# First batch's keys loaded by place and summed by matrix products; mean from an accumulated sum; idle products removed

## The chip, the cores and the metric

The kernel runs on one core of a Trainium2 chip. The metric is the time of one execution on the device in microseconds, the median of several runs; lower is better. The core's engines are named as the profile names them: PE (TensorE, matrix products), DVE (VectorE), ACT (ScalarE), POOL (GpSimd) and SP (SyncE, which here only issues transfers). Each takes its instructions strictly in the order of its own queue and waits for the others through semaphores.

## The reference

Attention over pooled keys, then a feed-forward network, both in float32:

```python
# q: 4 x 12288 x 128, kv: 4 x 384 x 32 x 128, w_sr: 128 x 128
kv_pool = kv.reshape(B, H // 4, 4, W // 4, 4, C).mean(axis=(2, 4))   # mean of 16 places
k = v = kv_pool.reshape(B, -1, C) @ w_sr                             # 768 keys a batch
s = scale * (q @ k.transpose(0, 2, 1))
a = np.exp(s - s.max(-1, keepdims=True))
a /= a.sum(-1, keepdims=True) + 1e-09
x = (a @ v).reshape(B * S, 128)
# w_in: 128 x 2048, w_out: 2048 x 128
h = x @ w_in
out = (h - np.tanh(h)) @ w_out
```

## The kernel before

The 49152 tokens are taken in 96 groups of 512, 24 to a batch. Channels lie on the 128 partitions. A group has 52 products of 512 columns on PE: six scores (L850), two shares (L878), three and six that make the weighted values (L884, L894), then sixteen forth into the 2048 inner features (L965), three linear terms (L954) and sixteen back (L1003). DVE and ACT turn each 128x1024 block of scores or inner features into its nonlinear part (L854, L857, L969, L972); one block a group is done by POOL (L979, L983). POOL also splits numbers into upper and lower parts (L888, L908, L934) and issues transfers that add (L873). ACT writes the group's result (L1014).

Ahead of the first group stands a head, which is the place of the change:

- `words_of` (L303) turns blocks of w_in and w_out, which arrive as 64-bit words, into float32: per block, three passes on ACT (L333, L349, L352) and four on DVE (L336, L339, L343, L355). Four blocks are of w_in, four of w_out.
- `weights` transposes w_in by products with the identity (L384), copies it (L392), and multiplies it with itself (L403, L407) for a bound that is only used at the end.
- `keys(b, s0)` (L425) makes the pooled keys of batch b. For batch 0, twelve transfers of 512 KB bring 64 keys with all 16 places each (L452). DVE sums the places of eight of these blocks (L466), POOL of four, by four halving additions (L460). The sums land in `kvp` (128x768). Six small sums per batch (L502), a sum over them (L506) and a scaling (L507) give the mean key; `apart` subtracts it (L511, ACT); `centre` multiplies it with w_sr (L514, PE; L517, DVE); `product` and `product_by_key` multiply the keys with w_sr, once by channel (L521) and once by key (L530); ACT copies the outcomes (L526, L543, L534); L547 is the values' second moment. For batches 1 to 3, POOL gathers the sums with adding transfers (L437) while the batch before is computed.
- `warm` (L488) multiplies parts of `kvp` with the identity; nothing reads the outcome.
- `about_centre` (L578) expands the network around the mean: sixteen products of one column (L614), a chain of small DVE instructions on `hb` (L619 to L670), then weights scaled by the parts of `hb`: `Wg` (L732, L756, DVE and POOL), products with them (L738, L763), copies on ACT (L746, `winr`), and `Wr` (L776, POOL). The first product forth (L965) needs `winr` and the first group's `dr` (L908).

The order of all instructions is made when the program is built: class `Plan` takes each piece of work with a step and a guessed duration, and repeatedly takes the piece that its model would start first, the lower step first among those that start together. `MOVES` (L222) shifts single steps of the head and of the next batches' work; `AT` (L806) holds the steps of a group's instructions. `HELD` names the pooling step of batch 0 from which the loads of w_out and of the first queries may be issued. `BUFS` gives the number of buffers behind each name; a tile that takes a buffer waits for all readers of the old one.

Of the kernel before, what the change touches and what calls it, by code (L numbers as in the profile page):

```python
# [15 lines left out]
AF = mybir.ActivationFunctionType  # L16
# [185 lines left out]
def attention_then_ffn(ctx: ExitStack, tc: tile.TileContext, q, kv_by_key, kv_by_place, w_sr, w_in,  # L202
# [5 lines left out]
    K, W = kv_by_key.shape[1], kv_by_key.shape[2]  # L208
# [31 lines left out]

    DIRECT, HELD = 2, 6
# [182 lines left out]

    def keys(b, s0):  # L425
# [6 lines left out]
        NK = K // KB  # L432
        c = min(b, 2)
        for w in range(W if b else 0):
            def gather(w=w):
                if w:
                    PL.dma_start(out=plan[kvp], in_=kv_by_place[b - 1, w], accum_op=ALU.add)  # L437
                else:
                    SP.dma_start(out=plan[kvp], in_=kv_by_place[b - 1, w])

            put = at((b * NG - GATHER[b - 1] + max(w - 1, 0)) * UN - 17.0, "gather", c, w)
            plan.op(put - (0.01 if w else 4), *(("POOL", 0.88) if w else ("SP", 0.5)), gather, (), (kvp,),
                    late=0.81 if w else 1.0, dma=2.3 if w else 1.1)
        for j in range(0 if b else NK):
            gap = 0.1
            s, key = s0 - gap * (NK - j) - 2, f"kc.{b}.{j}"
            sb(key, ("E", "r", "rp", "kc", "r", "r")[j % 6], [P, KB, W])
            ks = slice(j * KB, (j + 1) * KB)
            s = at(s, "pool", j)

            def load(ks=ks, key=key):
                SP.dma_start(out=plan[key], in_=kv_by_key[:, ks, :])  # L452

            plan.op(s - 8, "SP", 0.5, load, (), (key,), late=2.0, dma=1.27)
            if j % 3 == 2:
                for k, w in enumerate((8, 4, 2, 1)):
                    def fold(key=key, w=w, ks=ks):
                        x = plan[key]
                        to = plan[kvp][:, ks].unsqueeze(2) if w == 1 else x[:, :, 0:w]
                        PL.tensor_tensor(out=to, in0=x[:, :, 0:w], in1=x[:, :, w : 2 * w], op=ALU.add)  # L460

                    plan.op(s + k / 8, "POOL", 0.2 + KB * w * 0.0021, fold, (key,),
                            ((kvp, j),) if w == 1 else (key,))
            else:
                def pool(key=key, ks=ks):
                    V.tensor_reduce(out=plan[kvp][:, ks], in_=plan[key], op=ALU.add, axis=AX.X)  # L466

                plan.op(s, "DVE", 1.2, pool, (key,), ((kvp, j), "held") if j == HELD else ((kvp, j),))
# [13 lines left out]
        for x, put in ((pc, sc), (pm, s3), (p4, s4)):  # L482
            bank(x, "x", put)
        if b == 0:
            big("warm", s0 - 3)
            for j in range(WN // KB - 1, NK):
                def warm(j=j):
                    PE.matmul(out=plan["warm"][:, 0:WN], lhsT=ident,  # L488
                              rhs=plan[kvp][:, (j + 1) * KB - WN : (j + 1) * KB], start=True,
                              stop=True)  # L490

                plan.op(s0 - 3, "PE", 1.2, warm, ["ident"] + [(kvp, i) for i in range(j + 1)],
                        ("warm",))
        big(pk, s1)
# [810 lines left out]
```

## Time and profile before

| | us |
|---|---|
| median of 3 runs | 1290.07 |
| lowest and highest | 1289.26, 1292.4 |
| the profiled execution's own time | 1289.32 |
| its span, first to last instruction | 1287.6 |
| first product forth (L965) starts, from the span's start | 59.70 |
| the 96 group results (L1014) start | 78.7 to 1281.0 |

The span has a head of about 60 us, in which the weights and the first batch's keys are made ready, a long body of groups, and some 6 us behind the last result. The views used below are the page (one line for each engine), windows (busy time of each engine in a stretch and the clock that TensorE was granted; 1.00 is 2.4 GHz, 0.5 is 1.2 GHz), the list of waits, and timelines. In a timeline, neighbouring instructions of one line stand in one row with their count; the bracket says how long the engine stood idle ahead and for what. A matmul of float32 operands has two records for each product, so x16 is eight products.

### The profile page before, as it was taken

Reading aid. Unit: us, or ns where it says so; the run is one execution under the profiler, and the core shown is the slowest. Engines: PE = TensorE matmul, PEld = TensorE weight load, DVE = VectorE, ACT = ScalarE, POOL = GpSimd, SP = SyncE. Lnnn points to the kernel's source line nnn. Section 1 sums busy time; section 2 is a strip of 40 time slices with the busy share of each in tenths; the row PEclk is TensorE's granted clock in tenths of the full one; section 3 lists DMA queues with packets and bytes.
Section 4 is the critical chain, followed back from the end, with each engine's and each line's share of the span. In section 5 each row is a group of like instructions: output and inputs, shape, how many; then the busy total and the mean of one; then the engine's idle time right before and its main releaser. Section 6 shows DMA issues by size and latency. Waiting matters only on the chain.

```text
span 1287.6 us, 17375 instructions
## 1 busy us (share of the span) xinstructions
PE 1257.1 (98%) x5520; PEld 879.8 (68%) x5520; DVE 1213.7 (94%) x1201; ACT 1201.0 (93%) x1423; POOL 1147.5 (89%) x969
## 2 busy tenths in 40 slices
PE   5899999999999999999999999999999999999997
PEld 4666667777676677777766667776776666666665
DVE  6899899999999999999999999999999999999996
ACT  4799999999999999999999999999999999999995
POOL 3599987999999988899999987899988988989886
PEclk8999999999999999999999999999999999999999
DMA  9367744456657543455467743444434444344431
GB/s 364 69 144 151 167 98 107 111 127 148 143 132 161 120 118 90 125 131 138 108 148 143 160 103 103 103 119 107 115 90 115 103 106 118 93 115 103 106 88 33
DMA packets 82708, 158.46 MB, mean 123 GB/s; under 512 B 9937, under 2 KB 12113, under 8 KB 82609
## 3 DMA queue, kind: packets, MB, share of 16 engines
q0 software_dynamic: 33552, 66.99, 30.7%
q1 hardware_dynamic: 49056, 90.29, 20.0%
q8 instruction: 45, 0.74, 0.2%
q14 instruction: 55, 0.44, 0.1%
HBM read 57.93 MB, written 25.39 MB: 65 GB/s over the span
## 4 chain that ended last, share of the span: by engine, by line
PE 74%; POOL 14%; DMA 4%; issue 2%; DVE 2%; ACT 2%; SPq 0%; POOLq 0%; ACTq 0%; DVEq 0%
PE big L965 23%; PE acc L1003 22%; PE big L850 8%; PE x L894 8%; PE acc L954 4%; PE x L884 4%; DMA rs<-r 3%; POOL rp L983 3%; PE x L878 3%; POOL z L983 2%; POOL z L979 2%; POOL rs L873 2%; POOL ql L888 1%; POOL dl L934 1%; DVE r L972 1%
## 5 line engine op out<-in xcount | busy, mean ns | idle before, releaser
L972 DVE SCALAR_TENSOR_TENSOR r<-big,u 128x1024 fp32r<-128x1024 f32 x672 | 788.7, 1218 | 26.8 <-ACT u L969 26.4
L969 ACT ACTIVATE u<-big 128x1024 f32<-128x1024 f32 x672 | 671.1, 1029 | 34.8 <-PE big L965 23.3
L965 PE MATMUL big<-dr,winr 128*128 128x512 f32 x1536 | 518.9, 419 | 0.7 <-DVE r L972 0.6
L1003 PE MATMUL acc<-r,Wr 128*128 128x512 f32 x1344 | 414.5, 398 | 0.6 <-DVE r L972 0.6
L857 DVE SCALAR_TENSOR_TENSOR r<-E,big 128x1024 f16<-128x1024 f32 x288 | 350.2, 1217 | 22.5 <-ACT E L854 21.8
L965 PEld LDWEIGHTS big<-dr,winr 128*128 128x128 f32 x1536 | 272.1, 188 | 118.8 <-DVE r L972 33.0
L854 ACT ACTIVATE E<-big 128x1024 f32<-128x1024 f32 x288 | 297.2, 1033 | 3.7 <-PE big L850 2.5
L1003 PEld LDWEIGHTS acc<-r,Wr 128*128 128x128 f32 x1344 | 250.0, 188 | 58.5 <-DVE r L972 1.5
L983 POOL TENSOR_TENSOR rp<-z,v 128x1024 fp32r<-128x1024 f32 x96 | 270.8, 2821 | 0.2
L983 POOL TENSOR_TENSOR z<-z,v 128x1024 f32<-128x1024 f32 x96 | 243.8, 2539 | 0.1
L873 POOL DMA_DIRECT2D rs<-r x188 | 211.2, 1124 | 7.6 <-DMA rs<-r 6.1
L979 POOL TENSOR_SCALAR z<-v 128x1024 f32<-128x1024 f32 x96 | 122.7, 1278 | 82.1 <-ACT v L976 81.8
L850 PE MATMUL big<-qr,kTr 128*128 128x512 f32 x576 | 193.0, 417 | 0.4 <-ACT winr L746 0.2
L888 POOL TENSOR_TENSOR ql<-q,qr 128x512 fp32r<-128x512 f32 x96 | 185.2, 1929 | 1.1 <-ACT qr L835 1.1
L894 PE MATMUL x<-r,vvr 128*128 128x512 f16 x576 | 174.3, 385 | 0.0
L934 POOL TENSOR_TENSOR dl<-df,dr 128x512 fp32r<-128x512 f32 x96 | 163.2, 1700 | 0.0
L850 PEld LDWEIGHTS big<-qr,kTr 128*128 128x128 f32 x576 | 101.4, 188 | 39.9 <-DVE r L972 21.9
L976 ACT COPY v<-big 128x1024 f32<-128x1024 f32 x96 | 97.5, 1016 | 8.1 <-PE big L965 1.6
L894 PEld LDWEIGHTS <-vvr 128*128 128x128 f16 x576 | 33.4, 98 | 78.6 <-issue 78.4
L908 POOL TENSOR_SCALAR dr<-df 128x512 fp32r<-128x512 f32 x96 | 81.4, 848 | 0.0
L1003 PE MATMUL acc<-rp,Wr 128*128 128x512 f32 x192 | 77.0, 482 | 3.6 <-POOL rp L983 3.6
L1014 ACT ACTIVATE o<-acc,At 128x512 f32<-128x512 f32 x96 | 65.6, 683 | 7.5 <-PE acc L1003 7.4
(184 smaller groups left out, 1029.9 us busy)
## 6 DMA issues: line engine op xcount, KB each, us to landing
rs<-r POOLq DMA_DIRECT2D x188, 256.0 KB, 3.6
q<-in_q_dram SPq DMA_DIRECT2D x96, 256.0 KB
out_dram<-o SPq DMA_DIRECT2D x96, 256.0 KB
rs<-r SPq DMA_DIRECT2D x94, 256.0 KB
kvp<-in_kv_by_place_dram POOLq DMA_DIRECT2D x45, 384.0 KB, 6.0
r<-in_kv_by_key_dram SPq DMA_DIRECT2D x6, 512.0 KB
kc<-inverse SPq DMA_DIRECT2D x12, 256.0 KB
u<-in_moe_w_in_dram SPq DMA_DIRECT2D x3, 512.0 KB
```

What stands on the lines that cost most here:

```text
L850: PE.matmul(out=half(plan[s], h), lhsT=plan[kTr][:, n * P : (n + 1) * P], rhs=plan[qr], start=True, stop=True)
L854: A.activation(out=plan[e], in_=plan[s], func=AF.Exp)
L857: V.scalar_tensor_tensor(out=plan[r], in0=plan[e], scalar=-1.0, in1=plan[s], op0=ALU.add, op1=ALU.subtract)
L873: PL.dma_start(out=plan[rs], in_=plan[r2s[k]], accum_op=ALU.add)
L888: PL.tensor_tensor(out=plan[ql], in0=plan[qs], in1=plan[qr].bitcast(F32), op=ALU.subtract)
L894: PE.matmul(out=plan[num], lhsT=plan[vvr][:, n], rhs=half(plan[f"r2.{g}.{k}"], h), start=(start and h == 0), stop=(stop and h == 1))
L934: PL.tensor_tensor(out=plan[dl], in0=plan[df], in1=plan[dr].bitcast(F32), op=ALU.subtract)
L965: PE.matmul(out=half(plan[hp], h), lhsT=plan[winr][:, f * P : (f + 1) * P], rhs=plan[dr], start=True, stop=True)
L969: A.activation(out=plan[u], in_=plan[hp], func=AF.Square)
L972: V.scalar_tensor_tensor(out=plan[r], in0=plan[hp], scalar=1.0, in1=plan[u], op0=ALU.add, op1=ALU.mult)
L983: PL.tensor_tensor(out=plan[to], in0=plan[x], in1=plan[y], op=ALU.mult)
L1003: PE.matmul(out=plan[acc], lhsT=plan[Wr][:, 2 * n + h], rhs=half(plan[r], h), start=(start and h == 0), stop=(stop and h == 1))
```

## The change

For batch 0, the input that lay by key is gone; all four batches lie by place. Sixteen transfers of 384 KB bring one place of all 768 keys each, into buffers lent from other names (`PLACES`). DVE adds the first fourteen places in seven pairs (128x768); PE multiplies the seven sums and the last two places with w_sr, all into the same accumulator, nine products of 768 columns as two of 384. `sums` copies the outcome to `kvp` on ACT and accumulates its sum in the same instruction; three DVE scalings make from it the subtrahends and the centre. So `centre` and its copy are gone for batch 0, `apart` and `copy_keys` subtract by their bias, and the values by key come from products with the identity. POOL's halving additions and the products of `warm` are gone. For batches 1 to 3, one sum over 768 columns takes the place of six small ones and the sum over them. `HELD` goes from 6 to 3, and all numbers of `MOVES` and `AT` are new.

```diff
@@ -220,25 +220,23 @@
     MOVES = {
-        "load.i.0": -22.9, "load.i.1": -18.7, "words.i.1": -54.5, "words.i.3": -7.3, "WW": -172.2,
...
+        "words.o.0": 22.9, "words.o.2": -7.3, "words.o.3": 19.1, "first.0.3": 53.8,
...
-    DIRECT, HELD = 2, 6
+    DIRECT, HELD = 2, 3
@@ -422,6 +420,8 @@
+    PLACES = ("r", "r", "r", "r", "rp", "rp", "kc", "kc", "z", "E", "u", "u", "u", "E", "r", "r")
@@ -429,43 +429,44 @@
-        for j in range(0 if b else NK):
...
-            def load(ks=ks, key=key):
-                SP.dma_start(out=plan[key], in_=kv_by_key[:, ks, :])
...
-            if j % 3 == 2:
...
-                        PL.tensor_tensor(out=to, in0=x[:, :, 0:w], in1=x[:, :, w : 2 * w], op=ALU.add)
...
-                def pool(key=key, ks=ks):
-                    V.tensor_reduce(out=plan[kvp][:, ks], in_=plan[key], op=ALU.add, axis=AX.X)
...
+        ALONE = W - 2
+        for w in range(0 if b else W):
+            place = f"place.{w}"
+            sb(place, PLACES[w], [P, K])
+
+            def load(w=w, place=place):
+                SP.dma_start(out=plan[place], in_=kv_by_place[0, w])
...
+        for j, w in enumerate(() if b else [*range(0, ALONE, 2), *range(ALONE, W)]):
+            x, y = f"place.{w}", f"place.{w + 1}"
...
+            def add(x=x, y=y):
+                V.tensor_tensor(out=plan[x], in0=plan[x], in1=plan[y], op=ALU.add)
+
+            def place_product(x=x, w=w):
+                for c in range(2):
+                    PE.matmul(out=plan[pk][:, c * G : c * G + KH], lhsT=wsr,
+                              rhs=plan[x][:, c * KH : (c + 1) * KH], start=(w == 0),
+                              stop=(w == W - 1))
...
@@ -480,32 +481,29 @@
-        if b == 0:
-            big("warm", s0 - 3)
-            for j in range(WN // KB - 1, NK):
-                def warm(j=j):
-                    PE.matmul(out=plan["warm"][:, 0:WN], lhsT=ident,
-                              rhs=plan[kvp][:, (j + 1) * KB - WN : (j + 1) * KB], start=True,
-                              stop=True)
...
-        def part(n):
-            of = plan[kvp][:, n * 2 * KB : (n + 1) * 2 * KB].rearrange("p (a k) -> p a k", a=4)
-            V.tensor_reduce(out=plan[row][:, 4 * n : 4 * n + 4], in_=of, op=ALU.add, axis=AX.X)
...
+        def sums():
+            if b:
+                V.tensor_reduce(out=plan[row][:, 24:25], in_=plan[kvp], op=ALU.add, axis=AX.X)
+            else:
+                A.activation(out=halves(plan[kvp]), in_=key_halves(), func=AF.Identity,
+                             accum_out=plan[row][:, 24:25])
 
         def mean():
...
+            for to, by in ((25, -1.0 / K), (26, -scale / (K * W)), (27, 1.0 / (K * W)))[: 1 if b else 3]:
+                V.tensor_scalar(out=plan[cen] if to == 27 else plan[row][:, to : to + 1],
+                                in0=plan[row][:, 24:25], scalar1=by, scalar2=None, op0=ALU.mult)
@@ -522,13 +520,16 @@
         def copy_keys():
...
+                A.activation(out=halves(plan[kTr]), in_=key_halves(), func=AF.Identity,
+                             bias=plan[row][:, 26:27], scale=scale / W)
...
-                          rhs=wsr, start=True, stop=True)
+                          rhs=wsr if b else ident, start=True, stop=True)
...
@@ -804,14 +810,14 @@
     AT = dict(
-        forth=[4.5, 6.4, 3.4, 2.2, 5.4, 5.7, 0.3, 2.8],
...
+        forth=[4.6, 6.0, 5.2, -0.1, 1.2, 0.44, 5.6, -0.5],
...
```

On PE, between the transposes of w_in and the first second-moment product, there stands before (`big<-kvp,ident` is `warm`, `acc<-col,win` the first-order products):

```order
L384 MATMUL big<-ident,win_67 128x128 x16
L403 MATMUL x<-winT 128x128 x16
L488 MATMUL big<-kvp,ident 128x512 x4
L514 MATMUL x<-row,wsr 128x1
L488 MATMUL big<-kvp,ident 128x512
L614 MATMUL acc<-col,win_67 128x1 x8
L416 MATMUL x<-W_208 128x128
L530 MATMUL big<-wsr,kvp 128x128 x3
L521 MATMUL big<-kvp,wsr 128x384 x2
L614 MATMUL acc<-col,win_67 128x1 x8
L850 MATMUL big<-qr,kTr 128x512 x2
L530 MATMUL big<-wsr,kvp 128x128 x3
```

and now, with the sums and single places in the buffers r, rp, kc, z and u:

```order
L382 MATMUL big<-ident,win_67 128x128 x8
L463 MATMUL big<-r,wsr 128x384 x4
L463 MATMUL big<-rp,wsr 128x384 x2
L463 MATMUL big<-kc,wsr 128x384 x2
L463 MATMUL big<-z,wsr 128x384 x2
L463 MATMUL big<-u,wsr 128x384 x4
L463 MATMUL big<-r,wsr 128x384 x4
L620 MATMUL acc<-col,win_67 128x1 x12
L531 MATMUL big<-ident,kvp 128x128 x3
L382 MATMUL big<-ident,win_67 128x128 x8
L856 MATMUL big<-qr,kTr 128x512 x2
L620 MATMUL acc<-col,win_67 128x1 x4
L531 MATMUL big<-ident,kvp 128x128 x3
L401 MATMUL x<-winT 128x128 x16
```

Half of the transposes and the product of w_in with itself stand behind the first-order products now, and four of the sixteen first-order products behind transposes and scores.

On DVE, from the scaling of the mean to the instruction that takes over the first-order products (L619 before, L625 after; `v`, `wout` and `o` are the words of w_out), there stands before:

```order
L517 TENSOR_SCALAR col<-x 128x1
L339 TENSOR_SCALAR v<-v 128x512
L343 SCALAR_TENSOR_TENSOR wout_69<-u,v 128x512
L355 ISA wout_69<-wout_69,o 128x1024
L419 TENSOR_REDUCE norms<-x 128x1
L336 TENSOR_SCALAR v<-v 128x512
L339 TENSOR_SCALAR v<-v 128x512
L343 SCALAR_TENSOR_TENSOR wout_69<-u,v 128x512
L336 TENSOR_SCALAR v<-v 128x512
L355 ISA wout_69<-wout_69,o 128x1024
L339 TENSOR_SCALAR v<-v 128x512
L619 TENSOR_SCALAR hb<-acc 128x16
```

and now:

```order
L505 TENSOR_SCALAR row<-row 128x1 x2
L505 TENSOR_SCALAR col<-row 128x1
L334 TENSOR_SCALAR v<-v 128x512
L337 TENSOR_SCALAR v<-v 128x512
L341 SCALAR_TENSOR_TENSOR wout_69<-u,v 128x512
L334 TENSOR_SCALAR v<-v 128x512 x2
L337 TENSOR_SCALAR v<-v 128x512 x2
L341 SCALAR_TENSOR_TENSOR wout_69<-u,v 128x512 x2
L353 ISA wout_69<-wout_69,o 128x1024
L334 TENSOR_SCALAR v<-v 128x512
L353 ISA wout_69<-wout_69,o 128x1024
L625 TENSOR_SCALAR hb<-acc 128x16
```

Before, two blocks of w_out are whole ahead of the `hb` row and a third is begun; now three are taken up to their third pass, two of them whole, and a fourth is begun.

On POOL, from the first `Wg` to the first group's `dr`, there stands before:

```order
L756 TENSOR_TENSOR Wg<-winT,hb 128x4x128
L732 TENSOR_TENSOR Wg<-ident,hb 128x4x128
L555 TENSOR_TENSOR Mh<-Mn,Mh 128x128
L732 TENSOR_TENSOR Wg<-ident,hb 128x4x128
L776 TENSOR_TENSOR Wr<-wout_69,hb 128x512
L437 DMA kvp<-in_kv_by_place_dram 128x768
L756 TENSOR_TENSOR Wg<-winT,hb 128x4x128 x3
L776 TENSOR_TENSOR Wr<-wout_69,hb 128x512
L437 DMA kvp<-in_kv_by_place_dram 128x768
L776 TENSOR_TENSOR Wr<-wout_69,hb 128x512
L908 TENSOR_SCALAR dr<-df 128x512
```

and now:

```order
L762 TENSOR_TENSOR Wg<-winT,hb 128x4x128
L782 TENSOR_TENSOR Wr<-wout_69,hb 128x512 x3
L738 TENSOR_TENSOR Wg<-ident,hb 128x4x128
L556 TENSOR_TENSOR Mh<-Mn,Mh 128x128
L436 DMA kvp<-in_kv_by_place_dram 128x768
L738 TENSOR_TENSOR Wg<-ident,hb 128x4x128
L762 TENSOR_TENSOR Wg<-winT,hb 128x4x128 x2
L782 TENSOR_TENSOR Wr<-wout_69,hb 128x512
L436 DMA kvp<-in_kv_by_place_dram 128x768
L762 TENSOR_TENSOR Wg<-winT,hb 128x4x128
L914 TENSOR_SCALAR dr<-df 128x512
```

Three of the four `Wr` blocks stand ahead of the diagonal `Wg` (`Wg<-ident,hb`) now, and one `Wg<-winT,hb` directly ahead of `dr`; no `Wr` stands behind `dr`.

## Rows read from the trace of the kernel before

**Rows 1.** the page: busy time (share) xinstructions, and the chain by engine.

```profile
PE 1257.1 (98%) x5520; PEld 879.8 (68%) x5520; DVE 1213.7 (94%) x1201; ACT 1201.0 (93%) x1423; POOL 1147.5 (89%) x969
...
PE 74%; POOL 14%; DMA 4%; issue 2%; DVE 2%; ACT 2%; SPq 0%; POOLq 0%; ACTq 0%; DVEq 0%
```

**Rows 2.** windows: busy of PE, PEld, DVE, ACT, POOL; then PEclk, DMA, GB/s.

```profile
10.00:20.00 10.00, 8.31 (x61) 7.82 (x60) 8.66 (x14) 4.41 (x7) 6.08 (x8) 1.00 1.03 418
...
19.00:23.00 4.00, 0.03 (x1) 0.00 (x0) 3.11 (x3) 0.27 (x1) 2.80 (x5) 1.00 1.03 421
23.00:30.00 7.00, 6.30 (x8) 2.70 (x9) 3.40 (x10) 1.85 (x3) 3.75 (x5) 0.51 1.07 389
...
40.00:43.50 3.50, 3.27 (x14) 3.17 (x15) 3.33 (x11) 1.58 (x5) 0.03 (x1) 0.51 0.21 81
...
1010.00:1240.00 230.00, 230.00 (x981) 159.15 (x980) 226.00 (x208) 225.32 (x262) 202.99 (x163) 1.00 0.42 104
```

**Rows 3.** PE's waits, whole span: total us, times, longest.

```profile
PE acc L1003 <- POOL rp L983: 3.6, 5, 1.1
PE x L547 <- ACT kc L534: 1.9, 1, 1.9
PE acc L763 <- DVE wout L355: 0.7, 1, 0.7
```

**Rows 4.** the 96 group results, line L1014: duration, first and last start.

```profile
L1014 ACT ACTIVATE o<-acc,At x96: 678/682/703, 78.7 to 1281.0; 128x512 f32<-128x512 f32 x96
```

**Rows 5.** PE's timeline: start, us, engine, line, operation, [idle before <-releaser].

```profile
13.40 2.05 PE L384 MATMUL big<-ident,win 128*128 128x128 f32 x16 [0.71 <-DVE win L355]
15.29 3.74 PE L403 MATMUL x<-winT 128*128 128x128 f32 x32
...
23.70 6.72 PE L488 MATMUL big<-kvp,ident 128*128 128x512 f32 x8 [4.67 <-DVE kvp L466]
...
31.33 1.84 PE L614 MATMUL acc<-col,win 128*128 128x1 f32 x16
...
34.01 1.46 PE L521 MATMUL big<-kvp,wsr 128*128 128x384 f32 x4
...
40.23 2.93 PE L547 MATMUL x<-kc 128*128 128x128 f32 x12 [1.85 <-ACT kc L534]
...
57.90 2.05 PE L763 MATMUL acc<-Wg,wout 128*128 128x129 f32 x16 [0.70 <-DVE wout L355]
59.70 1.19 PE L965 MATMUL big<-dr,winr 128*128 128x512 f32 x4
```

**Rows 6.** DVE's timeline, same columns.

```profile
27.90 0.29 DVE L502 TENSOR_REDUCE row<-kvp 128x4 f32<-128x128 f32 x1 [2.45 <-POOL kvp L460]
...
28.43 0.15 DVE L507 TENSOR_SCALAR row<-row 128x1 f32<-128x1 f32 x1
...
37.18 0.17 DVE L619 TENSOR_SCALAR hb<-acc 128x16 f32<-128x16 f32 x1 [0.42 <-PE acc L614]
...
37.60 0.17 DVE L639 TENSOR_TENSOR hb<-hb 128x16 f32<-128x16 f32 x1
...
56.08 0.69 DVE L905 TENSOR_TENSOR df<-x,t 128x512 f32<-128x512 f32 x1
```

**Rows 7.** POOL's timeline, same columns.

```profile
24.96 2.53 POOL L460 TENSOR_TENSOR r<-r 128x512 f32<-128x512 f32 x3 [3.01 <-DMA r<-in_kv_by_key_dram]
...
56.26 1.03 POOL L776 TENSOR_TENSOR Wr<-wout,hb 128x512 fp32r<-128x512 f32 x1 [1.85 <-DVE wout L355]
57.27 1.05 POOL L908 TENSOR_SCALAR dr<-df 128x512 fp32r<-128x512 f32 x1
```

**Rows 8.** ACT's timeline, same columns.

```profile
26.25 0.68 ACT L333 ACTIVATE v<-u 128x512 f32<-128x512 f32 x1 [6.92 <-DMA u<-in_moe_w_out_dram]
...
31.53 0.94 ACT L511 ACTIVATE kvp<-kvp,row 128x768 f32<-128x768 f32 x1 [2.69 <-PE big L488]
...
35.83 0.79 ACT L526 ACTIVATE kTr<-big 128x768 fp32r<-128x768 f32 x1
```

More of the change, by code (lines that the diff above doesn't have):

```diff
@@ L207, in attention_then_ffn @@
     B, C, N = q.shape
[L208 removed]
+    W, K = kv_by_place.shape[1], kv_by_place.shape[3]
     F = w_in.shape[1]
@@ new lines, in keys @@
+        ALONE = W - 2
[4 more added lines that the diff above has]
+                SP.dma_start(out=plan[place], in_=kv_by_place[0, w])
+            plan.op(s0 - 12 + w / 16, "SP", 0.5, load, (), (place,), late=2.0, dma=0.95)
+        if b == 0:
+            big(pk, s0 - 3)
+        for j, w in enumerate(() if b else [*range(0, ALONE, 2), *range(ALONE, W)]):
+            x, y = f"place.{w}", f"place.{w + 1}"
+            put = at(s0 - 2 + j / 16, "pool", j)
+            def add(x=x, y=y):
[5 more added lines that the diff above has]
+                              stop=(w == W - 1))
+            if w < ALONE:
+                plan.op(put, "DVE", 0.87, add, (y,), (x, "held") if j == HELD else (x,), port=True)
+            plan.op(s0 - 2 + j / 16, "PE", 1.3, place_product, ("wsr", x), (pk,), late=0.2)
@@ L482, in keys @@
         for x, put in ((pc, sc), (pm, s3), (p4, s4)):
-            bank(x, "x", put)
-        if b == 0:
-            big("warm", s0 - 3)
-            for j in range(WN // KB - 1, NK):
-                def warm(j=j):
-                    PE.matmul(out=plan["warm"][:, 0:WN], lhsT=ident,
-                              rhs=plan[kvp][:, (j + 1) * KB - WN : (j + 1) * KB], start=True,
-                              stop=True)
-                plan.op(s0 - 3, "PE", 1.2, warm, ["ident"] + [(kvp, i) for i in range(j + 1)],
-                        ("warm",))
-        big(pk, s1)
+            if b or x != pc:
+                bank(x, "x", put)
+        if b:
+            big(pk, s1)
         big(pv, s2)
@@ L556, in moment_left @@
                              op=ALU.subtract)
-        for n in range(NK // 2):
-            of = (kvp,) if b else ((kvp, 2 * n), (kvp, 2 * n + 1))
-            plan.op(sc - 0.5, "DVE", 0.3, partial(part, n), of, ((row, n),))
-        plan.op(sc, "DVE", 0.35, mean, (row,), (row,))
-        plan.op(sc, "ACT", 0.85, apart, (kvp, row), (kvp,), late=0.1)
-        plan.op(sc, "PE", 0.2, centre, ("wsr", row), (pc,), late=0.2)
-        plan.op(sc, "DVE", 0.12, copy_centre, (pc,), (cen,))
-        for c in range(2):
-            plan.op(sv[0] if c else s1, "PE", 0.65, partial(product, c), ("wsr", kvp), ((pk, c),), late=0.2)
-        plan.op(sv[0], "ACT", 0.9, copy_keys, (pk,), (kTr,), late=0.1)
+        if b:
+            plan.op(sc - 0.5, "DVE", 0.87, sums, (kvp,), (row,))
+            plan.op(sc, "DVE", 0.12, mean, (row,), (row,))
+            plan.op(sc, "ACT", 0.85, apart, (kvp, row), (kvp,), late=0.1)
+            plan.op(sc, "PE", 0.2, centre, ("wsr", row), (pc,), late=0.2)
+            plan.op(sc, "DVE", 0.12, copy_centre, (pc,), (cen,))
+            for n in range(2):
+                plan.op(sv[0] if n else s1, "PE", 0.65, partial(product, n), ("wsr", kvp), ((pk, n),),
+                        late=0.2)
+            plan.op(sv[0], "ACT", 0.9, copy_keys, (pk,), (kTr,), late=0.1)
+        else:
+            plan.op(sc, "ACT", 0.85, sums, (pk,), (kvp, (row, 0)), late=0.1)
+            plan.op(sc, "DVE", 0.4, mean, ((row, 0),), ((row, 1), cen), late=0.1)
+            plan.op(sv[0], "ACT", 0.9, copy_keys, (pk, row), (kTr,), late=0.1)
+            plan.op(at(sc, "apart"), "ACT", 0.85, apart, (kvp, row), (kvp,), late=0.1)
         for j in range(2):
-            plan.op(sv[1] if j else s2, "PE", 0.7, partial(product_by_key, j), ("wsr", kvp), ((pv, j),),
+            plan.op(sv[1] if j else s2, "PE", 0.7, partial(product_by_key, j), ("wsr" if b else "ident", kvp), ((pv, j),),
                     late=0.2)
@@ L806, in attention_then_ffn @@
     AT = dict(
-        forth=[4.5, 6.4, 3.4, 2.2, 5.4, 5.7, 0.3, 2.8],
-        first=[3.7, 6.2, 2.3, -0.8, 5.0, 5.8, -1.2, 1.38],
-        then=[-4.8, 10.1, 6.0, 3.7, 9.5, 10.0, 2.4, 5.4],
-        back=[11.5, 11.0, 7.1, 6.3, 10.16, 10.3, 5.6, 6.46], scores=[-20.8, -19.0, -20.4],
-        exps=[-22.6, -20.0, -21.2], beyond=[-18.5, -15.0, -17.6], values=[-4.7, -4.5, -3.3],
-        more=[-2.2, -1.7], num=-5.0, copied=16.8, added=[-26.1, -22.4], shares=-5.6, left=-8.4,
-        straight=-3.6, apart=-0.6, rounded=-11.8, rounded_q=-25.5, slope=5.0, result=10.5,
-        lower_q=-21.6, lower_left=-6.6)
+        forth=[4.6, 6.0, 5.2, -0.1, 1.2, 0.44, 5.6, -0.5],
+        first=[3.78, 5.9, 4.6, -0.6, 1.4, 0.7, 5.8, -1.8],
+        then=[-7.6, 8.9, 8.4, 2.5, 3.8, 2.9, 8.5, 0.91],
+        back=[9.9, 8.5, 7.86, 5.6, 7.4, 6.1, 8.2, 5.22], scores=[-21.23, -19.2, -23.4],
+        exps=[-21.2, -20.2, -23.2], beyond=[-19.6, -16.1, -20.3], values=[-3.2, -6.4, -7.1],
+        more=[-5.0, -2.9], num=-6.9, copied=-7.6, added=[-27.1, -24.8], shares=-7.6, left=-7.33,
+        straight=-3.9, apart=-1.61, rounded=-14.8, rounded_q=-25.9, slope=4.9, result=9.41,
+        lower_q=-24.5, lower_left=-9.6)
     def attention(g, s0):
```

46 lines of the change are left out of this document (13 added, 33 removed), and 30 rows, old and new, of the table MOVES.

## The prediction

> **What bounds the kernel now.** I read the page's busy line first: PE is busy for 98% of the span and carries 74% of the chain that ended last [rows 1]. The window from 1010 to 1240 us then shows that this is a true bound in the body: PE is busy for all 230.00 us at a granted clock of 1.00, with DVE at 226.00 and ACT at 225.32 close behind [rows 2]. The list of waits confirms it: over the whole span, PE's waits inside the body sum to little, the largest entry being 3.6 us in five waits for POOL's `rp` [rows 3]. So between the first result at 78.7 and the last at 1281.0 [rows 4] nothing is to be won but those few microseconds, unless PE gets fewer products. It does not: the change keeps all 52 products of a group. What can move is the head, up to the first product forth at 59.70 [rows 5].
>
> In the head I followed the timelines. PE transposes and squares w_in up to 15.29 + 3.74 = 19.03, stands idle for 4.67 us and then runs `warm` [rows 5], while the keys come in at 418 GB/s [rows 2]. The last block of keys reaches POOL at 24.96, after 3.01 us of waiting for the transfer, and POOL needs 2.53 us and a last small addition for it [rows 7]; DVE then waits 2.45 us for POOL and sums the last part at 27.90 [rows 6]. The mean, `centre` and its copy follow, and the first-order products start at 31.33 [rows 5]. `hb` is taken at 37.18 [rows 6]. So the keys' transfer, POOL's folding and the serial path of the mean set the start of the chain, and `warm` stands beside it.
>
> **The change part by part.**
>
> *Transfers.* Twelve times 512 KB and sixteen times 384 KB are the same 6.3 MB. At 418 GB/s [rows 2] a place takes 393216 / 418000 = 0.94 us. I therefore put the last place where the last block was, at about 25.0, and the last but one at 24.0. The buffers fit this: the queue brings place 14 ahead of place 13, so that the seventh pair is complete only with the last transfer but one.
>
> *Pair additions.* No 128x768 addition is in the trace. A 128x512 one took 0.69 us (L905) and a 128x16 one 0.17 (L639) [rows 6]; the slope, 0.52 us for 496 columns, gives 0.17 + 752 x 0.00105 = 0.96 us. A pair arrives every 1.9 us, so DVE keeps up, and only the last addition counts: 24.0 to 25.0.
>
> *Products.* A product of 768 columns took 1.46 us in the trace, first start to last end (L521) [rows 5]. The sum of pair seven and the two single places stand in this order in PE's queue, so three products lie behind 25.0, even though place 14 was there earlier. At 1.3 to 1.46 each they end at 28.9 to 29.4; I take 29.0, since products that follow closely overlap. These nine products replace L521 and the ten records of `warm`.
>
> *The mean.* `sums` on ACT is a 128x768 pass: 0.94 us for L511, 0.79 for L526 [rows 8]; I take 0.94, to 30.0. No accumulating pass is in the trace; I bound it by one row of the same size and by twice that (1.9 us). Three scalings at 0.15 each (L507) [rows 6] and a start to start of about 0.2 bring the centre at 30.6, and the first-order products at 30.7, where they were at 31.33. Gain: 0.6 us. POOL's folds, the six small sums, `centre` and its copy are thus gone from this path, but three products and an ACT pass have come in.
>
> *From there to `hb`.* Sixteen records (eight products) took 1.84 us [rows 5], so twelve products take 2.8, to 33.5. Then PE has three value products, eight transposes (2.05 for sixteen records [rows 5]) and a pair of scores ahead of the last four: I get 37.5 for the accumulator. But DVE's queue now has three blocks of w_out ahead of the `hb` row, and these blocks' ACT passes begin only behind `sums`, for the first of them stands behind it in ACT's queue and its transfer stands behind four loads of queries. From about 30.7, ten ACT passes at 0.55 to 0.9 a step and then two DVE passes of 0.69 give 38.3 (38.0 to 38.8). So `hb` comes 1.1 us later than at 37.18, although the mean came 0.6 earlier. Behind the waiting DVE stands everything of `hb`, and POOL and PE wait for that.
>
> *From `hb` to the first product forth.* Before, this took 59.70 - 37.18 = 22.5 us. In it POOL's `Wr` waits 1.85 us for a block of w_out, `dr` ends at 58.32 [rows 7], and PE then still has most of sixteen records of L763 (2.05 us) to do, which had waited 0.70 for another block [rows 3, 5]. Now a third block of w_out is already done before `hb`, `Wr` no longer stands late, and only half of those sixteen records (about 1.0 us) stands ahead of the first product forth; the other half has gone behind it. Between getting nothing back (+1.1: 60.8) and getting back all of the 1.0 and the 1.85 (58.0), I take 59.4, nearer to the middle, because `dr` also rests on exponentials and DVE passes that are as many as before. Net: -0.3 us.
>
> *Behind the first product forth.* Eight records of the slopes' products have moved here: +1.0 us, since PE is the bound here. The waits for `rp` sit in the first groups, where POOL issues two adding transfers in a group; now the groups with two lie partly there and partly in the middle of the batch. Bounds: all 3.6 us gone [rows 3], or as much again lost; I take 0. For batches 1 to 3, seven small DVE instructions (six of some 0.29, one of 0.18) become one of at most 0.96 us, so DVE has 0.9 us less per batch in a body where PE never waits [rows 2]; I take -0.4 in all, between 0 and -2.7.
>
> *Sum.* -0.3 + 1.0 + 0.0 - 0.4 = +0.3 us on the profiled execution's 1289.32 us, that is 1289.6. The median of the runs is 0.75 above that execution, so the forecast means "no change".
>
> **TensorE's clock without `warm`.** After PE had done next to nothing from 19 to 23 us (0.03 us busy), its granted clock in the next window is 0.51, the lower of the two levels, and it is 0.51 again from 40 to 43.5, where a wait of 1.85 us for ACT had just ended [rows 2, 3, 5]. So a short idle time can cost the full clock. In the changed head PE has products from about 14 us on, one for each 1.9 us at 1.3 to 1.46, that is some 70% of the time, and then a gap from 29.0 to 30.7. The Trainium skill ("TensorE: Matmul & The Clock Gate", section "HAM oscillation — how this bites in real kernels") describes a loop whose bursts of products are shorter than the wait for the next data, and which found the throttle on again at every burst. By that rule all nine products would run at the lower level; here the bursts are longer than the waits, so I hold it for unlikely, and take the sum at the full clock up to 29.0.
>
> **The rivals.**
>
> *Clock lost at the end of the keys (slower).* Place: the last three products and the first-order products. At the lower level four 512-column products took 6.72 us (L488) [rows 5], so 768 columns take 1.5 x 1.68 = 2.52 us, and three of them 3.6 us more than at 1.3. Twelve first-order products would take up to 2.8 us more, of which 0.8 hides behind DVE's words. It decides when the clock falls before about 25 us: +3.6 to +5.6, so 1293.2 to 1295.2; if it only falls in the gap at 29, +2, so 1291.6. For it speak the two windows at 0.51, against it that PE's longest idle time ahead of 25 us should be some 1.5 us. With all nine products at the lower level, 14.4 + 9 x 2.52 = 37.1 instead of 29.0: +8, 1297.7, which is where the rule named above leads.
>
> *The body's waits go, and the head comes out short (faster).* If POOL's new order takes away the 3.6 us of waits for `rp`, and the head gets back what I called possible (58.0), the time is 1289.6 - 3.6 - 1.4 = 1284.6. For it speaks that DVE and POOL have less to do; against it that the transfers which POOL issues are as many.
>
> *POOL's pairs of transfers in mid-batch (slower).* Each new group with two of them could hold `rp` back by 0.7 us, the mean of the five waits [rows 3]. Five such groups cost +3.5: 1293.1. Against it: in the full window POOL is busy for only 203 of 230 us [rows 2].
>
> *The change does not do what it says.* If transfers of many small buffers go slower, say 389 instead of 418 GB/s [rows 2], the last place comes 1.0 us later: 1290.6. This counts as no change.
>
> **How the numbers follow.** Forecast and near variants, with the transfer case: 0.55. Clock lost: 0.19, of which about 0.12 lands above the bound, 0.03 of it the case of all nine. Waits gone: 0.18, nearly all of it faster. Pairs in mid-batch: 0.08, half above the bound. A measurement of this kernel can tell about 0.3% from no change, that is 3.9 us: faster below 1286.2, slower above 1293.9. Faster 0.20, same 0.63, slower 0.17. The range goes from the low rival, 1284.6, to the clock's upper case without the nine, 1295.0.
>
> **What would show it.** Right: adds of about 0.96 us on DVE, the last ending near 25; three products behind it with a PE clock of 1.00; the first-order products near 30.7; `hb` near 38.3, behind a pass of the words; the first product forth near 59.4; 95 periods between first and last result as long as before, 1281.0 - 78.7 = 1202.3. Wrong, if the clock in the windows from 14 to 31 us is near 0.5, if the accumulating pass takes near 1.9 us, if `rp` waits stand in the middle of a batch, or if the periods of the body differ by more than 2 us in sum.

## The result and the profile after

The changed kernel is slower: 1303.59 us (median of 6 runs, 1302.64 to 1304.74) against 1291.02 us for the kernel before in the same comparison, a ratio of 1.0099 with a 95% interval of 1.0086 to 1.0112. The forecast was "no change", 1289.6 us with a range up to 1295.0; the time lies above it. The profiled execution took 1303.50 us, its span is 1301.7 us.

The page's busy line, and the row of the 96 results (L1020 now, to set beside [rows 4]):

```profile
PE 1265.2 (97%) x5540; PEld 885.0 (68%) x5540; DVE 1210.0 (93%) x1176; ACT 1204.2 (93%) x1425; POOL 1136.8 (87%) x953
```

```profile
L1020 ACT ACTIVATE o<-acc,At x96: 675/683/693, 79.4 to 1295.1; 128x512 f32<-128x512 f32 x96
```

The first result comes at 79.4 instead of 78.7, the last at 1295.1 instead of 1281.0. So of the 14 us between the two spans the head up to the first result holds 0.7 and the body, first result to last, 13.4 (1215.7 against 1202.3). POOL has less to do and is idle longer. PE's waits in the whole span (line, releaser, total us, times, longest), to set beside [rows 3]:

```profile
PE acc L1009 <- POOL rp L989: 11.0, 15, 1.6
PE big L382 <- DVE win L353: 10.3, 1, 10.3
PE acc L620 <- DVE col L505: 1.3, 1, 1.3
PE big L744 <- DVE r L863: 0.9, 1, 0.9
```

The waits for `rp` went from 3.6 us in five to 11.0 us in fifteen. That list counts only idle time, and it rests on ends of products that the profile models. Counted from start to start instead, each product against the median for the same pair of neighbours (delays over 0.15 us), the products of `rp` are late by about 5 us in 6 groups before and by about 20 us in 27 groups after. The difference, some 14 to 15 us, covers the whole loss of the body. Summed by groups, from the starts of the results:

| groups | before, us | after, us |
|---|---|---|
| 0 to 12 | 155.0 | 158.7 |
| 12 to 24 | 155.8 | 157.2 |
| 24 to 36 | 154.2 | 155.5 |
| 36 to 48 | 153.6 | 158.1 |
| 48 to 60 | 154.2 | 155.6 |
| 60 to 72 | 152.8 | 153.1 |
| 72 to 95 | 276.7 | 277.4 |

From group 60 on, where POOL gathers no more keys, the two hardly differ. So the loss seems to need the gathering transfers (e3 below tests it), and yet the order of PE's products in a group is, by their kind, the same as before. The way from one to the other shows in POOL's timeline of the first group behind 79 us, before first, then after (start, us, engine, line, operation, [idle before <-releaser]):

```profile
83.15 2.56 POOL L983 TENSOR_TENSOR z<-z,v 128x1024 f32<-128x1024 f32 x1
85.52 1.04 POOL L873 DMA_DIRECT2D rs<-r  x1
86.16 2.85 POOL L983 TENSOR_TENSOR rp<-z,v 128x1024 fp32r<-128x1024 f32 x1
```

```profile
84.02 2.87 POOL L989 TENSOR_TENSOR z<-z,v 128x1024 f32<-128x1024 f32 x1
89.40 0.89 POOL L879 DMA_DIRECT2D rs<-r  x1 [2.52 <-DMA rs<-r]
90.04 2.65 POOL L989 TENSOR_TENSOR rp<-z,v 128x1024 fp32r<-128x1024 f32 x1
```

A group has three `r2` blocks (128x1024, DVE's outcome of the scores), and `rs` is their sum: SP copies one of them to `rs`, and POOL issues two transfers that add the others. The first of these stands between the two multiplications that make `rp`. It must wait until SP's copy of the block `r2s[0]`, the first by number, has landed. After the change it waits 2.52 us for that, with `rp` behind it in the queue. The block that it adds, the last of the three, was done five microseconds earlier, at 84.25 (DVE's L863, 83.03 + 1.22). SP's queue says why the copy is late, again before and after:

```profile
79.45 0.36 SPq L1017 DMA_DIRECT2D out_dram<-o  x1
79.91 0.47 SPq L870 DMA_DIRECT2D rs<-r  x1
```

```profile
80.14 0.36 SPq L1023 DMA_DIRECT2D out_dram<-o  x1
82.31 0.47 SPq L876 DMA_DIRECT2D rs<-r  x1
```

Before, the copy follows the result's store at once. After, it stands 2.2 us behind it, because it waits for DVE. DVE's making of the first two blocks, before, then after:

```profile
78.05 1.21 DVE L857 SCALAR_TENSOR_TENSOR r<-E,big 128x1024 f16<-128x1024 f32 x1
...
80.38 1.22 DVE L857 SCALAR_TENSOR_TENSOR r<-E,big 128x1024 f16<-128x1024 f32 x1
```

```profile
78.49 1.21 DVE L863 SCALAR_TENSOR_TENSOR r<-E,big 128x1024 f16<-128x1024 f32 x1
...
81.06 1.22 DVE L863 SCALAR_TENSOR_TENSOR r<-E,big 128x1024 f16<-128x1024 f32 x1 [0.23 <-ACT E L860]
```

The new `AT` makes the third block of scores first (its `beyond` step is -20.3, that of the first block -19.6; before they were -17.6 and -18.5). `copied` still takes `r2s[0]`. Before, that was the block made first, ready at 79.26; now it is the group's second, ready at 82.28, and the copy is issued that much later. In a group without gathering transfers it mostly still lands in time; beside them it held POOL until 89.4.

In the head, PE's timeline after, to set beside [rows 5]:

```profile
25.58 2.74 PE L463 MATMUL big<-r,wsr 128*128 128x384 f32 x8
29.63 2.84 PE L620 MATMUL acc<-col,win 128*128 128x1 f32 x24 [1.30 <-DVE col L505]
32.33 0.91 PE L531 MATMUL big<-ident,kvp 128*128 128x128 f32 x6
33.08 3.35 PE L382 MATMUL big<-ident,win 128*128 128x128 f32 x16
...
60.57 1.18 PE L971 MATMUL big<-dr,winr 128*128 128x512 f32 x4
```

and the windows (busy us of PE, PEld, DVE, ACT, POOL, then granted clock, DMA share, GB/s):

```profile
19.00:23.00 4.00, 4.00 (x14) 2.27 (x12) 1.56 (x2) 0.00 (x0) 0.00 (x0) 1.00 1.03 413
23.00:30.00 7.00, 4.86 (x18) 2.57 (x16) 1.23 (x4) 2.16 (x5) 1.26 (x1) 1.00 1.07 392
30.00:40.00 10.00, 10.00 (x75) 9.86 (x75) 7.65 (x23) 8.84 (x15) 0.00 (x0) 0.83 0.26 84
```

The clock stays at 1.00 through all place products. It falls to 0.50 at 33.4 us, just after L382 has begun, and the sixteen records of L382 take 3.35 us, where sixteen such records took 2.05 before [rows 5].

### The profile page after: what moved, and what is told of

Read it like the earlier page. It is cut to its first block, busy times and chain, and to the rows that moved or that the text cites. A ratio compares the mean times of both kernels' runs of the same rounds, so it can differ in the third digit from the quotient of the medians.

```text
span 1301.7 us, 17390 instructions
## 1 busy us (share of the span) xinstructions
PE 1265.2 (97%) x5540; PEld 885.0 (68%) x5540; DVE 1210.0 (93%) x1176; ACT 1204.2 (93%) x1425; POOL 1136.8 (87%) x953
## 4 chain that ended last, share of the span: by engine, by line
PE 76%; POOL 10%; DVE 6%; DMA 3%; issue 2%; ACT 2%; SPq 0%; POOLq 0%; DVEq 0%; ACTq 0%
PE big L971 23%; PE acc L1009 22%; PE big L856 8%; PE x L900 8%; PE acc L960 4%; PE x L890 4%; POOL rp L989 4%; DVE r L978 3%; PE x L884 3%; DMA rs<-r 2%; POOL rs L879 2%; DVE r L863 2%; POOL z L989 1%; POOL z L985 1%; PE x L620 1%
## 5 line engine op out<-in xcount | busy, mean ns | idle before, releaser
L863 DVE SCALAR_TENSOR_TENSOR r<-E,big 128x1024 f16<-128x1024 f32 x288 | 350.2, 1217 | 35.2 <-ACT E L860 34.1
L971 PEld LDWEIGHTS big<-dr,winr 128*128 128x128 f32 x1536 | 272.9, 188 | 117.7 <-DVE r L978 30.7
L989 POOL TENSOR_TENSOR rp<-z,v 128x1024 fp32r<-128x1024 f32 x96 | 267.6, 2788 | 0.2
L989 POOL TENSOR_TENSOR z<-z,v 128x1024 f32<-128x1024 f32 x96 | 246.9, 2572 | 0.1
L879 POOL DMA_DIRECT2D rs<-r x188 | 205.8, 1095 | 31.7 <-DMA rs<-r 14.4
L940 POOL TENSOR_TENSOR dl<-df,dr 128x512 fp32r<-128x512 f32 x96 | 160.2, 1669 | 0.0
L1020 ACT ACTIVATE o<-acc,At 128x512 f32<-128x512 f32 x96 | 65.7, 684 | 18.2 <-PE acc L1009 16.7
```

The lines of the kernel that those rows point to most:

```text
L863: V.scalar_tensor_tensor(out=plan[r], in0=plan[e], scalar=-1.0, in1=plan[s], op0=ALU.add, op1=ALU.subtract)
L879: PL.dma_start(out=plan[rs], in_=plan[r2s[k]], accum_op=ALU.add)
L940: PL.tensor_tensor(out=plan[dl], in0=plan[df], in1=plan[dr].bitcast(F32), op=ALU.subtract)
L971: PE.matmul(out=half(plan[hp], h), lhsT=plan[winr][:, f * P : (f + 1) * P], rhs=plan[dr], start=True, stop=True)
L989: PL.tensor_tensor(out=plan[to], in0=plan[x], in1=plan[y], op=ALU.mult)
```

## The experiments

The theory to test, "late copy": the copy's later issue, together with the gathering transfers that slow its landing, holds POOL's queue and so `rp`. Against it stood that POOL is held by issuing the gathers themselves at their new places, that the traffic hurts whatever the copy does, and, for the head, what the missing idle products cost. Line numbers in the edited kernels are shifted.

**e1: the old `AT` in the changed kernel, nothing else.**

> The changed kernel with the group table AT of before; loads by place, products, mean and MOVES stay as changed. Theory (late copy): the new table makes the first r2 block of a group, which SP copies to rs, about 2 us later; POOL's adding transfer waits for that copy, and rp stands behind it in POOL's queue. Then the old table brings the waits of L1009 for rp from 11.0 down to 3 to 5 us, and the time to 1289 to 1294. Rival (POOL's occupancy: where MOVES puts the gathering transfers): the waits stay near 11 and the time at 1300 or more.

Measured: 1305.94 us, ratio 1.0091 (1.0074 to 1.0108). The waits for `rp` did as the theory said, the time did not:

```profile
PE acc L1009 <- POOL rp L989: 4.9, 6, 1.3
PE x L512 <- DVE row L505: 4.7, 2, 2.4
```

The new `MOVES` had been set to the new `AT`; with the old one the product of the next batches' centre comes before its mean is there. Groups 0 to 12 took 155.4 us, as in the kernel before (155.0; 158.7 in the changed one); the loss has moved to groups 24 to 36 and 48 to 60 (160.3 and 158.6), where a batch begins, and to the head (first result at 81.1). The table alone can't be judged by the time, since it moves everything else too.

**e4: the new `AT` in the kernel before, nothing else.**

> The kernel before with the group table AT of the changed kernel alone. Late copy: the waits for rp rise from 3.6 to 9 to 14 us, 1297 to 1304. Rival (POOL's occupancy by the places of the gathers, which stay as before): 1289 to 1292.

Measured: 1315.76 us, 1.0171 (1.0154 to 1.0188). The waits rise to the upper end of what was expected, and the head suffers as well, probably from the same mismatch (first result at 86.1); the time is above what either case had:

```profile
PE acc L1003 <- POOL rp L983: 13.7, 22, 1.4
...
PE big L965 <- POOL dr L908: 3.8, 2, 2.6
```

**e2: another block to copy, given to the planner.** `r2s[k]` became `r2s[(2, 1, 0)[k]]` in the copy and the additions, in the planner's dependencies too.

> The changed kernel, but SP copies the r2 block that is made first in a group (the third by number) to rs, and POOL adds the other two. Late copy: the copy is issued some 2 us earlier, the adding transfer no longer waits, rp waits fall to 5 us or less, 1291 to 1296. Rival (POOL's occupancy): nothing changes, 1301 to 1305.

Measured: 1313.30 us, 1.0147 (1.012 to 1.0175); `rp` 8.1 us in eleven waits, but 4.4 us of waiting for the centre and a longer head. The planner had changed the whole order, so this does not decide between the theories. After it, only emitted instructions were edited, with the order kept.

**f1: the same edit, order of every queue kept.**

```diff
-            SP.dma_start(out=plan[rs], in_=plan[r2s[0]])
+            SP.dma_start(out=plan[rs], in_=plan[r2s[TURN[0]]])        # TURN = (2, 1, 0)
-            PL.dma_start(out=plan[rs], in_=plan[r2s[k]], accum_op=ALU.add)
+            PL.dma_start(out=plan[rs], in_=plan[r2s[TURN[k]]], accum_op=ALU.add)
```

> The changed kernel with the order of every engine kept instruction for instruction; only the block that SP copies to rs is the group's r2 block made first (POOL adds the other two at the same places). Late copy: the copy is issued about 1.8 us earlier in each group, rp waits fall from 11.0 to 2 to 5 us and the body from 1215.7 to 1203 to 1208 us; 1293 to 1297. If what hurts is only the gathering traffic in the new places, whatever the copy: nothing changes, body 1214 to 1217.

Measured: 1297.22 us, 1.0033 (1.0023 to 1.0043): by the medians, two thirds of the loss are gone by exchanging which block is copied. The copy is now issued at 82.22, right behind the store at 81.76. The waits fell less than expected, to 7.6 us; the profiled execution was this kernel's slowest (1301.48), with the longest single wait, 2.1 us, in a stretch of lower clock (0.80 from 637 to 645 us). Its body took 1212.2 us, longer than the 1203 to 1208 that were expected: groups 0 to 12 are cured (153.7), groups 12 to 24 and 36 to 48 (158.7 and 160.3) are not.

```profile
PE acc L1011 <- POOL rp L991: 7.6, 13, 2.1
```

**f3: the mirror image in the kernel before.** Its tables and queues are kept; SP copies the block that is made second instead of first (and stands behind it).

> The kernel before, all tables and every queue's order kept; only the block that SP copies to rs is the r2 block made second in a group instead of the first, so that the copy is issued about 1.7 us later. Late copy: rp waits rise from 3.6 to 8 to 13 us, 1296 to 1303. Rival (the new tables act in another way, the copy does not matter): 1289 to 1292.

Measured: 1305.48 us, 1.0096 (1.0077 to 1.0116), and

```profile
PE acc L1016 <- POOL rp L996: 14.7, 18, 1.5
```

The kernel before, with this one exchange and nothing of the change, is as slow as the changed kernel; waits and time are even a little above what was expected. That settles that the copy's block is enough to make a loss of this size. It does not settle that it is all of the changed kernel's: f1 left a third, and how much of this third belongs to the gathers' new places and how much to the head no run separates.

**e3 and g2: the traffic taken away.** The gathering transfers move 8 of 768 columns (`out=plan[kvp][:, 0:8]`) in the changed kernel (e3) and in the one before (g2); the keys of batches 1 to 3 are therefore not summed.

> The changed kernel, but each adding transfer that gathers the keys of batches 1 to 3 moves 8 of the 768 columns, so that these keys are not summed; POOL issues as many transfers at the same places. Late copy, lengthened by the gathering traffic: rp waits fall to 0 to 2 us, 1288 to 1293. Rival (POOL's occupancy by issuing): the waits stay near 11 us, 1300 to 1304.

> The kernel before with gathering transfers of 8 instead of 768 columns, so that the keys of batches 1 to 3 are not summed. Late copy under traffic: the waits for rp in the first groups go from 3.6 to 0 to 1 us, 1285 to 1289, the same as the changed kernel with small gathers (1287.65), so that without the traffic the two kernels do not differ. Rival (the changed kernel has another loss in the body that the traffic does not make): 1281 to 1285, clearly faster than 1287.65.

Measured: 1287.65 us, 0.9960 (0.9946 to 0.9974), and 1284.08 us, 0.9945 (0.993 to 0.996). The waits for `rp`, e3 then g2:

```profile
PE acc L1009 <- POOL rp L989: 1.9, 3, 1.2
```

```profile
PE acc L1003 <- POOL rp L983: 1.4, 2, 0.8
```

POOL issues as many transfers as ever, and for no less time; only their landing is sooner. In the changed kernel and in e3 (duration ns min/median/max; us from issue to landing):

```profile
L436 POOL DMA_DIRECT2D kvp<-in_kv_by_place_dram x45: 865/1192/1786, 42.4 to 754.7; - x45
...
DMA to landing us min/median/max: 4.5/5.5/7.4
```

```profile
L436 POOL DMA_DIRECT2D kvp<-in_kv_by_place_dram x45: 859/1333/2021, 42.2 to 738.3; - x45
...
DMA to landing us min/median/max: 2.2/3.0/5.0
```

So it is the traffic, not POOL's issuing. Without it the two ratios differ by 0.0015, some 2 us, instead of 0.0099. g2 is below the range expected for it by a microsecond and inside that of its rival, another loss in the body. Its profile puts most of the difference in the head instead: the first result comes at 76.4 against 78.8 in e3, the bodies take 1198.3 and 1199.6.

**f2 and f5: `rp` ahead of the adding transfer** in POOL's queue, one exchange in each group, in the changed kernel (f2) and in the one before (f5).

> The changed kernel with one exchange in POOL's queue in each group: rp (the second product with v) ahead of the first adding transfer. Late copy holding POOL's queue: rp waits fall from 11.0 to 0 to 3 us, and the time to 1290 to 1297, where the shares (L884) may come to wait for rs, up to 5 us in all. If rp is late because POOL's own work (z, v) is late: waits stay above 8 us, 1300 or more.

> The kernel before with rp ahead of the first adding transfer in POOL's queue. Late copy: the 3.6 us of waits for rp fall to 0 to 1 and the time by 3 to 6 us, 1285 to 1288, faster than both kernels. Rival: the adding transfers come 2.7 us later, the shares wait for rs in their place, 1289 to 1296.

Measured: 1360.89 us, 1.052 (1.0498 to 1.0541), and 1365.36 us, 1.0561 (1.054 to 1.0581). Both expectations fell. POOL's and PE's waits in f2:

```profile
POOL rs L890 <- DMA rs<-r: 136.0, 88, 3.9
...
PE big L982 <- POOL dr L925: 38.9, 32, 4.2
```

The first addition now comes 2.7 us later, the second waits for its landing in nearly every group, and behind that one stands `dr`, which starts the next group. POOL's queue holds the additions where they have to be; what can be moved is the copy.

**g4: the copy ahead of the result's store** in SP's queue, in the kernel before.

> The kernel before with one exchange in SP's queue: the copy to rs ahead of the group's result store, so that it is issued about 0.5 us earlier in each group. Late copy: the waits for rp fall from 3.6 to 1 to 3 us, the time by 1 to 3 us, a little faster than before. If the margin is not set by the copy's issue: no change.

Measured: 1291.55 us, 0.9997 (0.9986 to 1.0008): no change, with 4.5 us of waits for `rp` in five. Half a microsecond earlier than the block made first is worth nothing that can be measured.

**f4, i1, i2, i3: the clock in the head.** f4, and i1 as its repetition, put six idle products of 128 columns into the 1.30 us gap ahead of L620; i2 also one behind each of the twelve first-order products; i3 is the changed kernel again.

```diff
         def first(n):
+            for k in range(0 if b or n else 6):
+                PE.matmul(out=plan[f"{ph}.0"][:, P : 2 * P], lhsT=wsr, rhs=ident, start=True, stop=True)
```

> The changed kernel with six idle products of 128 columns put back into PE's queue between the last place product and the first first-order product, where PE waits 1.30 us; nothing reads them. If the gap costs the clock: the granted clock from 30 to 40 us goes from 0.83 to 1.00, the sixteen records of L382 from 3.35 to about 2.1 us, hb (37.94) comes 1.0 to 1.3 us earlier, the time falls by 0.5 to 1.5 us against the changed kernel. If the clock is lost for another reason: no change of the clock, same time. Either way the waits for rp stay at 9 to 12 us: 1301.5 to 1303.5.

> The same kernel as f4 (changed kernel with six idle products in the gap), once more beside the changed kernel. If the gap costs the clock in most executions: 1 to 2 us less than i3, granted clock 1.00 from 30 to 40 us. If the clock falls at its own moments, whatever stands in the gap: the same as i3 within 1 us.

> As i1, with an idle product of 128 columns behind each of the first twelve first-order products of one column as well (some 1.3 us more on PE, ahead of the products that hb waits for). If it is the stretch of one-column products that lets the clock fall: clock 1.00 from 30 to 40 us, and about 0 to 1 us less than i3. If not: 1 us more than i1.

> The changed kernel itself, as the measure for i1 and i2 on the same chip: 0.8 to 1.2% above the kernel before; granted clock 0.7 to 0.9 from 28 to 40 us.

Measured: f4 1306.21 us, 1.0108 (1.0088 to 1.0128); i1 1303.36, 1.0086 (1.0071 to 1.01); i2 1305.59, 1.0106 (1.009 to 1.0121); i3 1306.83, 1.0117 (1.0102 to 1.0133). The window from 28 to 40 us in f4, then i1, i2 and i3:

```profile
28.00:40.00 12.00, 12.00 (x73) 11.41 (x72) 6.26 (x17) 8.98 (x14) 0.00 (x0) 0.72 0.37 131
```

```profile
28.00:40.00 12.00, 12.00 (x86) 11.40 (x85) 7.42 (x23) 9.69 (x15) 0.00 (x0) 0.86 0.39 139
```

```profile
28.00:40.00 12.00, 12.00 (x104) 11.63 (x103) 6.99 (x21) 9.27 (x15) 0.00 (x0) 1.00 0.35 125
```

```profile
28.00:40.00 12.00, 10.70 (x77) 10.35 (x77) 7.96 (x26) 10.41 (x17) 0.00 (x0) 0.86 0.37 129
```

With the gap filled the clock fell all the same in f4 (0.72) and i1 (0.86), though PE is recorded as busy for all 12.00 us; with wider products between those of one column it did not. That would point to the stretch of one-column products rather than to the gap, but it rests on one profile, and g5 and h2 below kept 1.00 with f4's idle products and no others. In time it comes to little: f4 does not differ from the changed kernel and lies above its range, i1 is 0.3% below i3, more than either of its cases had, and i2 0.1%. The waits for `rp` are those of the changed kernel or more: 12.7, 13.3, 11.8 and 12.9 us. What the clock does here from run to run stays open.

**g5: three repairs together** in the changed kernel: f1's block, g4's exchange, and the six idle products.

> The changed kernel with three repairs: the copy from the r2 block made first, the copy ahead of the result store in SP's queue, and six idle products in the gap. If the late copy and the clock are the two losses: rp waits 2 to 6 us, clock 1.00 from 30 to 40, 1290 to 1294, about even with the kernel before. If the places of the gathers hold a loss of their own: waits stay at 7 us or more, 1295 to 1298.

Measured: 1294.79 us, 1.0029 (1.0015 to 1.0042), `rp` 4.0 us in eight waits, and the clock as in this window:

```profile
28.00:40.00 12.00, 12.00 (x102) 11.57 (x101) 8.78 (x32) 11.38 (x19) 0.00 (x0) 1.00 0.46 161
```

The waits are those of the kernel before, the time, just above the range, is not quite. By its ratio it is no better than f1, so the exchange in SP's queue and the idle products added nothing that can be measured. Beside g4, the kernel before with the same exchange in SP's queue, its first result comes at 78.8 instead of 77.6 and its body takes 1206.7 instead of 1204.6 us.

**h1 and h2: gathers not pulled together.** The entries `gather.*` of `MOVES` taken out, in the kernel before (h1) and in g5 (h2).

> The kernel before without the entries of MOVES that pull single gathering transfers forward, so that POOL issues one in nearly every group from 1 to 9 where it issued two in groups 2, 3 and 5; the tables are otherwise kept, so the planner also moves the next batches' work. If two transfers in a group are what is left of the waits for rp: they fall from 3.6 to 0 to 1.5 us and the time by 2 to 4 us, a little faster than both kernels. If one transfer in a group is enough to make the copy late, or the next batch's keys now come late: waits of 3 us or more, or new waits for the keys; 1290 to 1296.

> The changed kernel with the three repairs (copy block made first, copy ahead of the store, idle products) and without the entries of MOVES that pull gathering transfers forward. If two transfers in a group hold the remaining 4.0 us of waits for rp: 1 to 3 us, 1290 to 1293, even with the kernel before. If not: 4 us or more, 1294 to 1298.

Measured: 1317.40 us, 1.0197 (1.0183 to 1.021), and 1346.01 us, 1.0411 (1.0395 to 1.0427). PE's waits in h1:

```profile
PE x L512 <- DVE row L505: 16.5, 1, 16.5
...
PE big L963 <- POOL winr L712: 9.4, 1, 9.4
...
PE acc L1001 <- POOL rp L981: 0.7, 2, 0.5
```

With one gathering transfer in nearly every group the waits for `rp` go from 3.6 to 0.7, as expected: there the groups with two hold what is left of them. But the keys then come too late for products that stand at fixed places in PE's queue, and that costs far more. In h2:

```profile
PE x L519 <- DVE row L512: 43.8, 3, 21.3
PE acc L1022 <- POOL rp L1002: 4.1, 6, 2.2
```

Here the waits for `rp` did not fall, against the expectation; the longest, 2.2 us, stands in a group in which POOL still issues three gathering transfers. No run here that sums all keys beat the kernel before.

## Why the prediction was wrong, by its own steps

- *The step that failed* is "behind the first product forth", the term for `rp`. It was taken as 0 with bounds of 3.6 us to either side; the products of `rp` came some 14 us later than before. The bounds came from the waits that the trace of before already had. They took the waits' number as given by the gathers' places, and did not ask what `rp` stands behind in POOL's queue. The change of `AT` was read for PE alone, "the change keeps all 52 products of a group", which held; that the blocks of scores were now made in another order, and that SP's copy hangs on one of them, was not followed up. The row for the copy's trigger was to be had (SP and DVE around 79 us). What the runs showed in its place: POOL waits for the late copy with `rp` behind it (2.52 us at a time), and the copy's block alone makes the loss in the kernel before (f3, +0.96%). One of the prediction's own signs of being wrong showed it: the body's periods differ by 13.4 us in sum, where it had allowed 2.
- The rival "POOL's pairs of transfers in mid-batch" had the right engine and the right victim, but was priced at five groups of 0.7 us. The waits came in 15 groups, group 1 among them, in which POOL issues one gathering transfer. The argument against this rival, that POOL is busy for only 203 of 230 us, did not count, since POOL stood idle behind a transfer.
- *The two small terms behind the first product forth*, +1.0 and -0.4: no run separates them from the waits.
- *Transfers, additions, products.* An addition took 0.95 us (estimate 0.96), the last ended at 24.14 (25.0); the last product ended at 28.32 (29.0). Right.
- *The mean.* `sums` took 0.81 us and 0.19 more to read out its sum (estimate 0.94); the first-order products began at 29.63 (30.7). Right, a little early.
- *To `hb`.* It came at 37.94 (38.3 forecast), but for another reason. DVE was not held by the words of w_out, whose last pass ended at 36.71; it waited 1.23 us for the accumulator, since PE ran L382 at the lower clock. In g5, at the full clock, `hb` came at 36.81. So the nearness of 37.94 to 38.3 is luck.
- *From `hb` to the first product forth.* 22.6 us, as long as before (22.5); I had taken 21.1. None of what was called possible came back: POOL now waited 2.15 us for PE to free a `Wg` buffer, the last `Wg` was ready only at 59.60, and the eight records of the slopes' products that need it still stood ahead. So the product began at 60.57 instead of 59.4. Moreover the profiled execution of before had a head longer than usual, with a clock of 0.72 from 19 to 31 us; in g2, g4 and f5, which share that head, the clock there was 0.86 and the first product forth came at 58.10 to 58.26. Against those the changed head is some 2 us longer (some 1 us in g5, at the full clock), not 0.3 shorter.
- *The clock of the place products.* 1.00 throughout, as the sum had it; PE's longest wait among them was 0.84 us. What the prediction drew from the Trainium skill ("TensorE: Matmul & The Clock Gate", section "HAM oscillation — how this bites in real kernels"), all nine products at the lower level, did not show. The clock fell later, at 33.4 us, nearly 4 us behind the gap at which the milder form of the first rival (+2) had it. That the gap causes it is not borne out: f4 and i1 lost the clock without the gap.

## What to carry to other kernels

Where a change comes with new tables of an order, follow each queue that a bound engine waits for back through its own queue to what it stands behind, and that to its trigger: the engine that does the work may be early while a transfer ahead of it waits. A transfer that is in time by a margin stays hidden only as long as the traffic beside it leaves the margin. And a table that fits one order can't be judged by exchanging it alone (e1, e4), nor a dependency by letting the planner order everything anew (e2); exchanging single instructions in a kept order (f1, f3) shows more.

## What the runs showed of the hardware that was not expected

- A 256 KB copy issued by SP at 82.31 beside a gathering transfer released its waiter only at 89.40, 7.1 us later; the same copy in the kernel before (79.91) held up nobody at 85.52, 5.6 us later.
- Cutting a gathering transfer from 768 to 8 columns brought its landing from 5.5 to 3.0 us (medians), while POOL's issuing took no less time (1.19 and 1.33 us).
- The granted clock fell while PE was recorded as busy for all of 12.00 us (i1, 0.86 from 28 to 40 us); it fell right behind 2.84 us of products of one column. In g5 and h2, with the same idle products, it did not fall.
- An activation that accumulates shows as two instructions, 0.81 us and a read-out of 0.19 us.
